# Attention of two batches ahead of all blocks, in rounds with three pairs under way, and the blocks of two chunks in alternation

## The chip, the cores and the metric

One core of a Trainium2 chip runs the program. The metric is the device time of one execution in microseconds (us), lower is better. "The second layer starts" is used below as a second, finer metric: it is the first matmul record of the second layer of chunk 0, up to which both kernels do the same work and after which their programs are alike.

In the views PE is TensorE (matmuls), PEld its weight loads, DVE VectorE, ACT ScalarE, and L159 is line 159 of that kernel, so the same statement can have another number in another kernel. PSUM is the memory into which all matmuls of this kernel write. "Half clock" means that the trace's record of the granted TensorE clock reads 0.50; in the two traces the record changes after 3.41 us or a multiple of it. The head pairs of attention go through steps that are called KV, Q, U, NORM and X below.

## The reference, cut to what matters

```python
def _attn_ref(q, k, v, g_norm):                 # batch 8, heads 8, seq 576, head_dim 64, fp32
    kv = np.einsum('bhsd,bhse->bhde', k, v)
    out = np.einsum('bhsd,bhde->bhse', q, kv)
    rms = np.sqrt(np.mean(out * out, axis=-1, keepdims=True) + 1e-06)
    return out / rms * g_norm

def _moe_ref(x, w_gate, w_val, w_out):          # x: 4608 x 512, d_ff 1536
    gate = 1.0 / (1.0 + np.exp(-(x @ w_gate)))
    return gate * (x @ w_val) @ w_out
```

The weights come as 64-bit floats. The kernel loads them as pairs of 32-bit words and converts them on the chip, unit by unit: 12 units of gate and value weights, 6 of output weights.

## The kernel before

Tokens are cut into chunks of 512. A chunk's first layer has 12 blocks (one for each 128 columns of d_ff), and a block (c, f) needs weight unit f. Chunk 0 needs the four head pairs of batch 0. Chunk 1 needs batch 1 as well. The code is shortened.

```python
def convert(u): return [s0, s1, s2, s3, s4, s5, s6]   # seven DVE steps for one weight unit; L159 is in s6;
                                                      # s2 also starts ACT's Abs of the next unit

def attention(n, at_ps):                              # one head pair, eleven steps
    # kv_mm (PE), kv_out (DVE, then load k, v of pair n+2), q_mm (PE transpose), q_out (ACT copy, then load q),
    # u_mm (PE), u_square (ACT), u_sum (DVE), u_root (ACT Sqrt), u_norm (DVE), x_mm (PE transpose), x_out (ACT)
    ...

load_unit(0)                                          # first loads
for n in range(2):
    load_kv(n)
    load_q(n, nc.scalar)
...
do(0, KV, KV_OUT, Q, Q_OUT)                           # batch 0: hardly two pairs under way
do(1, KV, KV_OUT, Q, Q_OUT)
load_unit(1)
do(0, U, U_SQUARE, U_SUM, U_ROOT, U_NORM)
do(2, KV, KV_OUT, Q, Q_OUT)
do(0, X, X_OUT)
...
for f in range(1, NHP + 2):                           # blocks (0,1)..(0,5), one pair of batch 1 inside each
    plain(0, f, 7, pair_steps(f - 1))
for f in range(NHP + 2, NFT):                         # then alternating, six units apart
    plain(0, f, 5, [[]] * 8)
    plain(1, f - NHP - 2, 5, [[]] * 8)
for f in range(NFT - NHP - 2, NFT - 3):
    plain(1, f, 8, [[]] * 8)
finish()
convert_some(len(converts))
second_layer(0, two, 2)
```

## Time and profile before

| | before |
|---|---|
| median of the runs beside the change | 1215.49 us (1212.87 to 1215.98, 4 runs) |
| PE busy | 1172.0 us, 97% of 1213.0 |
| PE idle before 113 us / from there to 220.6 us | 32.7 us / 0.1 us |
| second layer starts | 220.63 us |

A PE that is busy 97% of the time leaves little to gain, so the reader should ask where the other 3% lie, and where it is busy at half its clock. Both lie in the first 113 us (granted clock 0.91 from 14 to 51 us, 0.86 from 51 to 113, then 1.00). The lines for it are in the prediction.

### The profile page before, as it was taken

The numbers are of one execution on the slowest core, as the hardware profiler recorded it, in microseconds if no ns is written. First come the engines' busy times: TensorE is split into PE (matmuls) and PEld (weight loads), VectorE is DVE, ScalarE is ACT, GpSimd is POOL, SyncE is SP. The second block draws the span as 40 slices with busy tenths as digits, with TensorE's granted clock in tenths as the row PEclk, the third lists the DMA queues.
The fourth block names the chain that finished last, engine by engine and source line by source line (L and its number), as shares of the span: only waits on it lengthen the run. The fifth ranks groups of instructions, "written<-read, shape, count | busy, mean of one in ns | idle before, by whom it ended". The sixth has DMA issues, their size and how long they took to land.

```text
span 1213.0 us, 13391 instructions
## 1 busy us (share of the span) xinstructions
PE 1172.0 (97%) x5136; PEld 786.9 (65%) x5136; DVE 473.5 (39%) x845; ACT 308.5 (25%) x577; POOL 241.8 (20%) x342
## 2 busy tenths in 40 slices
PE   4788999999999999999999999999999999999998
PEld 4444444455478846885588648874888478748863
DVE  4667878303034412543045404540345125504430
ACT  3444121113033312431143203420334021101110
POOL 0000000100024401331044203330244015403410
PEclk9889999999999999999999999999999999999999
DMA  9544322131012101120211102110110000010000
GB/s 243 136 129 134 104 104 70 29 78 46 17 47 60 30 18 47 31 59 9 56 30 31 38 26 59 30 31 26 40 29 1 18 18 1 1 27 9 1 9 26
DMA packets 71582, 57.48 MB, mean 47 GB/s; under 512 B 40800, under 2 KB 65376, under 8 KB 71520
## 3 DMA queue, kind: packets, MB, share of 16 engines
q1 hardware_dynamic: 68992, 56.05, 17.0%
q10 hardware_dynamic: 2528, 0.59, 0.3%
q8 instruction: 41, 0.67, 0.2%
q14 instruction: 21, 0.17, 0.0%
HBM read 47.19 MB, written 9.44 MB: 47 GB/s over the span
## 4 chain that ended last, share of the span: by engine, by line
PE 93%; DVE 3%; ACT 2%; DMA 1%; issue 1%; ACTq 0%; SPq 0%; DVEq 0%
PE mm L489 42%; PE mm L321 23%; PE two L341 13%; PE two L321 7%; PE at L238 2%; PE two L238 2%; PE at L211 1%; PE at L264 1%; DVE sq L256 1%; PE at L224 1%; PE two L211 1%; DMA q<-in_q_dram 1%; ACT L251 1%; PE two L264 1%; DVE ms L247 1%; ACT sq L243 1%
## 5 line engine op out<-in xcount | busy, mean ns | idle before, releaser
L472 POOL TENSOR_TENSOR tw<-gv 128x256 f32<-128x256 f32 x168 | 120.4, 728 | 913.8 <-PE mm L489 691.5
L321 PE MATMUL mm<-wo,gv 128*128 128x512 f32 x672 | 290.5, 592 | 0.0
L489 PE MATMUL mm<-sx,tw 128*128 128x256 f32 x1008 | 234.2, 380 | 0.0
L321 PEld LDWEIGHTS mm<-wo,gv 128*128 128x128 f32 x672 | 127.3, 190 | 155.3 <-issue 155.0
L489 PEld LDWEIGHTS mm<-sx,tw 128*128 128x128 f32 x1008 | 188.8, 190 | 24.6
L341 PE MATMUL two<-xT,gv 128*128 128x512 f32 x384 | 176.7, 611 | 14.3 <-DVE gv L159 14.3
L501 DVE TENSOR_TENSOR gv<-mm,p 128x256 f32<-128x256 f32 x84 | 35.7, 425 | 321.2 <-PE mm L489 321.2
L489 PE MATMUL mm<-xT,gv 128*128 128x256 f32 x672 | 159.7, 380 | 1.2 <-ACT sg L326 1.2
L489 PEld LDWEIGHTS mm<-xT,gv 128*128 128x128 f32 x672 | 126.0, 190 | 21.2 <-issue 2.9
L341 PEld LDWEIGHTS two<-xT,gv 128*128 128x128 f32 x384 | 72.2, 195 | 98.2 <-issue 93.1
L472 POOL TENSOR_TENSOR tw<-gv,tw 128x256 f32<-128x256 f32 x168 | 126.2, 771 | 1.1
L321 PE MATMUL two<-wo,gv 128*128 128x512 f32 x192 | 84.6, 594 | 0.0
L326 ACT COPY sg<-mm 128x512 f32<-128x512 f32 x28 | 16.4, 585 | 264.5 <-PE mm L321 264.5
L510 DVE TENSOR_TENSOR gv<-mm,p 128x256 f32<-128x256 f32 x84 | 35.6, 424 | 114.3 <-PE mm L489 114.3
L489 PE MATMUL mm<-sx,gv 128*128 128x256 f32 x336 | 79.9, 381 | 0.0
L489 PE MATMUL mm<-xT,tw 128*128 128x256 f32 x336 | 79.9, 381 | 0.0
L519 ACT ACTIVATE sg<-sg 128x256 f32<-128x256 f32 x84 | 35.0, 417 | 162.9 <-DVE sg L518 161.6
L489 PEld LDWEIGHTS mm<-xT,tw 128*128 128x128 f32 x336 | 63.0, 190 | 8.5
L489 PEld LDWEIGHTS mm<-sx,gv 128*128 128x128 f32 x336 | 63.0, 190 | 8.5
L526 DVE TENSOR_TENSOR gv<-gv,sg 128x512 f32<-128x512 f32 x84 | 66.6, 832 | 0.2
L321 PEld LDWEIGHTS two<-wo,gv 128*128 128x128 f32 x192 | 35.8, 190 | 41.8 <-issue 41.6
L495 ACT COPY p<-mm 128x256 f32<-128x256 f32 x84 | 31.3, 372 | 93.5 <-PE mm L489 93.5
(67 smaller groups left out, 824.7 us busy)
## 6 DMA issues: line engine op xcount, KB each, us to landing
k<-in_k_dram SPq DMA_DIRECT2D x32, 288.0 KB, 3.5
v<-in_v_dram SPq DMA_DIRECT2D x32, 288.0 KB, 4.1
q<-in_q_dram SPq DMA_DIRECT2D x60, 144.0 KB, 3.1
st<-in_moe_w_gate_dram SPq DMA_DIRECT2D x12, 512.0 KB, 3.9
st<-in_moe_w_val_dram SPq DMA_DIRECT2D x12, 512.0 KB, 5.1
st<-in_moe_w_out_dram SPq DMA_DIRECT2D x12, 512.0 KB, 4.1
out_dram<-sg SPq DMA_DIRECT2D x24, 192.0 KB, 2.3
out_dram<-sg SPq DMA_DIRECT2D x24, 128.0 KB, 2.3
```

The costliest lines, as they stand in the source:

```text
L211: nc.tensor.matmul(ps[HD * e:HD * e + HD, 0, 0:HD], pairs[n]["k"][:, e, js], pairs[n]["v"][:, e, js], start=(j == 0), stop=(j == NJ - 1))
L238: nc.tensor.matmul(ps[0:NP, j // JH, c0:c0 + P], d["qT"][:, j // JH, NP * (j % JH):NP * (j % JH) + NP], kvs[n % 2], start=True, stop=True)
L264: nc.tensor.transpose(ps[:, j // JH, c0:c0 + NP], d["xn"][:, j // JH, P * (j % JH):P * (j % JH) + P], ident[0:NP, 0:NP])
L321: nc.tensor.matmul(ps[:, i], gv[c, f][:, ts], w["wo", f], start=(f == 0), stop=(f == NFT - 1))
L341: nc.tensor.matmul(self.ps[:, i], w[("wg", "wv")[i], self.f][:, m, :], xT[self.c][:, m, :], start=(m == 0), stop=(m == NMT - 1), skip_grou ...
L472: nc.gpsimd.tensor_tensor(out=tw[f, i], in0=b[in0], in1=b[in1] if isinstance(in1, tuple) else tw[f, in1], op=ALU.subtract)
L489: nc.tensor.matmul(ps, wt[:, m, :], xs[:, m, :], start=(new and m == 0), stop=(m == NK - 1), skip_group_check=True)
L495: nc.scalar.copy(out=d["p1"], in_=pa)
L501: tt(out=d["h"][:, h1], in0=pb, in1=d["p1"], op=ALU.add)
L510: tt(out=d["h"][:, h2], in0=pb, in1=d["p1"], op=ALU.add)
L519: nc.scalar.activation(out=d["sg"][:, h2], in_=d["sg"][:, h2], func=AF.Sigmoid)
L526: tt(out=d["h"], in0=d["h"], in1=d["sg"], op=ALU.mult)
```

## The change

The intent is to take the weight conversion out of PE's way. The attention of batches 0 and 1 is done first, in rounds in which three pairs are under way, from PSUM buffers of its own. Then the blocks of chunks 0 and 1 alternate, so that one weight unit serves two blocks in a row. The first loads are reordered too.

```diff
+    load_kv(0)
+    load_q(0)
     load_unit(0)
-    for n in range(2):
-        load_kv(n)
-        load_q(n, nc.scalar)
+    load_kv(1)
+    load_q(1)
 ...
+    def early(kind):
+        shape, bufs = {"kv": ([P, 1, 512], 2), "qx": ([P, 2, 512], 1), "u": ([P, 2, 512], 2)}[kind]
+        return psum_e.tile(shape, FP32, tag=kind, name=kind, bufs=bufs)
 ...
+    def stage(i, n_convert):
+        do(i, KV, KV_OUT, Q, Q_OUT)
+        do(i - 2, U_SUM, U_ROOT, U_NORM)
+        do(i - 3, X, X_OUT)
+        do(i - 1, U, U_SQUARE)
+        ...
+    for i in range(NE + 1):
+        stage(i, 3 if i < 2 else 1 if i == 2 else 0)
+    blk = Plain(0, 0, early("u"))
+    for m in range(NMT):
+        blk.mm(0, m)
+    take_abs(1)
+    stage(NE + 1, 1)
+    for m in range(NMT):
+        blk.mm(1, m)
+    stage(NE + 2, 1)
+    blk.gate()
+    convert_some(1)
+    blk.end()
+    psum_ctx.__exit__(None, None, None)
     psum0_ctx = tc.tile_pool(name="psum0", bufs=4, space=bass.MemoryType.PSUM)
 ...
-    for f in range(1, NHP + 2):
-        plain(0, f, 7, pair_steps(f - 1))
-    ...
+    plain(1, 0, 7)
+    for f in range(1, NFT - 3):
+        plain(0, f, 6)
+        plain(1, f, 6)
+    for f in range(NFT - 3, NFT):
+        plain(0, f, 6)
```

More of the change, by code (lines that the diff above doesn't have):

```diff
@@ L71, in load_kv, with load_q @@
             pairs[n][name] = t
-    def load_q(n, queue=None):
+    def load_q(n):
         if n >= B * NHP:
@@ L78, in load_q @@
         for e in range(2):
-            (queue or nc.sync).dma_start(out=t[:, :, e, :], in_=q[b, h0 + e].rearrange("(p j) d -> p j d", j=NJ))
+            nc.sync.dma_start(out=t[:, :, e, :], in_=q[b, h0 + e].rearrange("(p j) d -> p j d", j=NJ))
         pairs[n]["q"] = t
@@ L206, in kv_mm @@
         def kv_mm():
-            d["kv"] = ps = at_ps()
+            d["kv"] = ps = at_ps("kv")
             for j in range(NJ):
@@ L220, in q_mm @@
         def q_mm():
-            d["q"] = ps = at_ps()
+            d["q"] = ps = at_ps("qx")
             for j in range(NJ):
@@ L232, in u_mm @@
         def u_mm():
-            ps = at_ps()
+            ps = at_ps("u")
             d["u"] = ps[0:NP, :, 0:JH * P]
@@ L260, in x_mm @@
         def x_mm():
-            d["x"] = ps = at_ps()
+            d["x"] = ps = at_ps("qx")
             for j in range(NJ):
@@ L327, in second_layer, with two, __init__ @@
                 store(c, t0 + i, ot)
-    def two():
+    def two(kind=None):
         return psum0.tile([P, 2, 512], FP32, tag="two", name="two")
+    def early(kind):
+        shape, bufs = {"kv": ([P, 1, 512], 2), "qx": ([P, 2, 512], 1), "u": ([P, 2, 512], 2)}[kind]
+        return psum_e.tile(shape, FP32, tag=kind, name=kind, bufs=bufs)
     class Plain:
-        def __init__(self, c, f):
-            self.c, self.f = c, f
-            self.ps = two()
+        def __init__(self, c, f, ps):
+            self.c, self.f, self.ps = c, f, ps
         def mm(self, i, m):
@@ L355, in finish, with plain @@
             late.popleft()()
-    def plain(c, f, n_convert, steps=None):
+    def plain(c, f, n_convert):
         converted(f)
-        blk = Plain(c, f)
+        blk = Plain(c, f, two())
         for at in range(2 * NMT):
@@ L363, in plain @@
             blk.mm(i, m)
-            if steps:
-                for step in steps[at]:
-                    step()
-            if steps is None:
-                slot()
+            slot()
             if late:
@@ L372, in plain, with do @@
         late.extend([blk.gate, blk.end])
+    KV, KV_OUT, Q, Q_OUT, U, U_SQUARE, U_SUM, U_ROOT, U_NORM, X, X_OUT = range(11)
+    psum_ctx = tc.tile_pool(name="psum_e", bufs=1, space=bass.MemoryType.PSUM)
+    psum_e = psum_ctx.__enter__()
+    NE = 2 * NHP
+    a = [attention(n, early) for n in range(NE)]
+    def do(n, *steps):
+        if 0 <= n < NE:
+            for step in steps:
+                a[n][step]()
+    def stage(i, n_convert):
[3 more added lines that the diff above has]
+        do(i - 1, U, U_SQUARE)
+        if i == 0:
+            take_abs(0)
+        convert_some(n_convert)
+        if i + 2 == NE:
+            load_unit(1)
+            load_unit(2)
@@ L374 @@
+    for i in range(NE + 1):
[12 more added lines that the diff above has]
+    psum_ctx.__exit__(None, None, None)
     psum0_ctx = tc.tile_pool(name="psum0", bufs=4, space=bass.MemoryType.PSUM)
     psum0 = psum0_ctx.__enter__()
-    a = [attention(n, two) for n in range(2 * NHP)]
@@ L378, in do @@
-    def do(n, *steps):
-        for step in steps:
-            a[n][step]()
-    KV, KV_OUT, Q, Q_OUT, U, U_SQUARE, U_SUM, U_ROOT, U_NORM, X, X_OUT = range(11)
-    take_abs(0)
-    converted(0)
-    do(0, KV, KV_OUT, Q, Q_OUT)
-    do(1, KV, KV_OUT, Q, Q_OUT)
-    load_unit(1)
-    do(0, U, U_SQUARE, U_SUM, U_ROOT, U_NORM)
-    do(2, KV, KV_OUT, Q, Q_OUT)
-    do(0, X, X_OUT)
-    do(1, U, U_SQUARE, U_SUM, U_ROOT, U_NORM)
-    do(3, KV, KV_OUT, Q, Q_OUT)
-    load_unit(2)
-    do(1, X, X_OUT)
@@ L395 @@
-    do(2, U, U_SQUARE, U_SUM, U_ROOT, U_NORM)
-    blk = Plain(0, 0)
-    for i in range(2):
-        blk.mm(i, 0)
-    do(2, X, X_OUT)
-    do(3, U, U_SQUARE, U_SUM, U_ROOT, U_NORM)
-    for m in (1, 2):
-        for i in range(2):
-            blk.mm(i, m)
-    take_abs(1)
-    do(3, X, X_OUT)
-    converted(1)
-    do(4, KV, KV_OUT, Q)
-    for i in range(2):
-        blk.mm(i, 3)
-    do(4, Q_OUT)
-    late.extend([blk.gate, blk.end])
-    def pair_steps(p):
-        n, o = a[NHP + p] if p < NHP else None, a[NHP + p - 1] if p else None
-        slots = [[] for _ in range(2 * NMT)]
-        if n:
-            if p:
-                slots[0] += [n[KV]]
-                slots[1] += [n[KV_OUT], n[Q]]
-                slots[2] += [n[Q_OUT]]
-            slots[3] += [n[U]]
-            slots[4] += [n[U_SQUARE]]
-            slots[5] += [n[U_SUM]]
-            slots[6] += [n[U_ROOT]]
-            slots[7] += [n[U_NORM]]
-        if o:
-            slots[2] += [o[X]]
-            slots[3] = [o[X_OUT]] + slots[3]
-        return slots
@@ L432 @@
-    for f in range(1, NHP + 2):
-        plain(0, f, 7, pair_steps(f - 1))
-    for f in range(NHP + 2, NFT):
-        plain(0, f, 5, [[]] * 8)
-        plain(1, f - NHP - 2, 5, [[]] * 8)
-    for f in range(NFT - NHP - 2, NFT - 3):
-        plain(1, f, 8, [[]] * 8)
+    plain(1, 0, 7)
[4 more added lines that the diff above has]
+        plain(0, f, 6)
     finish()
@@ L556, in mm_ps, with at_ps @@
         return psum.tile([P, 512], FP32, tag="mm", name="mm", bufs=6)
-    def at_ps():
+    def at_ps(kind):
         return psum.tile([P, 2, 512], FP32, tag="at", name="at")
```

## The prediction

> **What bounds the kernel now.** I read first the page: PE is busy 97% of 1213 us, so only the stretch where it is not can pay. The busy time by stage finds that stretch.
>
> ```profile
> 0.00:14.00 14.00, 2.70 (x30) 2.32 (x30) 5.66 (x9) 2.95 (x3) 0.70 (x6) 1.00 0.88 213
> 14.00:51.00 37.00, 26.59 (x209) 20.50 (x209) 18.76 (x31) 16.41 (x31) 0.00 (x0) 0.91 0.77 178
> 51.00:113.00 62.00, 50.98 (x232) 27.50 (x233) 42.42 (x56) 26.23 (x36) 0.00 (x0) 0.86 0.49 142
> 113.00:220.60 107.60, 107.54 (x253) 47.46 (x251) 89.16 (x96) 22.12 (x29) 1.72 (x3) 1.00 0.26 88
> 220.60:338.00 117.40, 116.83 (x433) 57.16 (x431) 15.45 (x28) 22.43 (x40) 3.88 (x6) 1.00 0.17 44
> ```
>
> Columns: stretch, length, busy time of PE, PEld, DVE, ACT, POOL, granted clock, DMA share, GB/s. PE idles 11.3 + 10.4 + 11.0 us before 113 us and nowhere after, and the clock is below full only there. Next, the timeline of PE gives prices and the moment at which I shall compare.
>
> ```profile
> 113.01 107.78 PE L341 MATMUL two<-xT,gv 128*128 128x512 f32 x250
> 220.63 1.88 PE L321 MATMUL two<-wo,gv 128*128 128x512 f32 x4
> 222.44 0.92 PE L211 MATMUL two<-v,k 96*64 96x64 f32 x24
> 223.29 3.70 PE L321 MATMUL two<-wo,gv 128*128 128x512 f32 x8
> 226.83 0.66 PE L224 MATMUL two<-ident,q 96*128 96x96 f32 x6
> 227.32 3.63 PE L321 MATMUL two<-wo,gv 128*128 128x512 f32 x8
> 230.78 1.47 PE L238 MATMUL two<-kv,qT 128*96 128x128 f32 x12
> 232.09 2.31 PE L321 MATMUL two<-wo,gv 128*128 128x512 f32 x5
> ```
>
> 250 records in 107.78 us are 0.431 us each; the code's 8 matmuls of a block are 16 records (384 for 24 blocks), so a block costs 6.90 us. From start to next start KV costs 0.85, Q 0.49, U 1.31 and the second transpose X the same as Q: 3.15 us a pair. Up to 220.63 us, where the second layer of chunk 0 begins, both kernels do the same PE work: 21 blocks (12 of chunk 0, 9 of chunk 1) and 8 pairs, 145 + 25 = 170 us. The kernel before wastes 50.5 us by then. After that point the programs are equal. So the question is only when this point comes.
>
> The waits of PE up to 330 us tell what it waits for:
>
> ```profile
> PE two L341 <- DVE gv L159: 14.3, 5, 3.2
> PE two L211 <- DMA v<-in_v_dram: 11.8, 2, 10.7
> PE two L264 <- DVE sq L256: 5.0, 4, 2.1
> ```
>
> L159 is the last of seven DVE steps that convert one weight unit; blocks 0 to 5 of chunk 0 each need a fresh unit, and DVE has attention to do as well. The other waits are the first loads and the latency of a pair's norm, since hardly two pairs are under way. They sum to 31 us; the rest of the 50.5, some 19, is chiefly half clock.
>
> [...] the granted clock falls to 0.91 and 0.86 just where PE has gaps; 24 KV matmuls take 1.55 us early and 0.92 later. [...] The trace has the switches, at 1.28 us each:
>
> ```profile
> 57.75 0.81 ACT L243 ACTIVATE sq<-two 96x768 f32<-96x768 f32 x1 [5.76 <-PE two L238]
> 58.57 1.28 ACT L251 ACT_TABLE_LOAD   x1
> 59.86 0.30 ACT L251 ACTIVATE ms<-ms,eps 96x12 f32<-96x12 f32 x1
> 60.19 1.28 ACT L346 ACT_TABLE_LOAD   x1
> 61.48 0.60 ACT L346 ACTIVATE sg<-two 128x512 f32<-128x512 f32 x1
> ```
>
> [...] q moves in pieces of 256 B; the trace shows only 223 to 259 GB/s between 10 and 40 us with its DMA share at 1. I use 240 GB/s for pairs and 330 for weight units.
>
> **The change, part by part.**
>
> (1) *Loads reordered.* k, v, q of pair 0 come before the first weight unit. A pair is 864 KB, 3.6 us; a unit 1.05 MB, 3.2 us. Data flows from 2 us. Pair 0 is there by 6, its KV and Q run (cold) until 8.6; then unit 0 to 9.0 and pair 1 to 12.6[...]. Since U of pair 0 stands behind KV and Q of pair 1 in PE's order, the gain of the start is partly lost: round 1 runs from 13 to 18 us at half clock.
>
> (2) *Rounds.* A round is KV, Q, X of three pairs ago, U of the last. The one buffer for Q and X makes PE wait for the ACT copy of Q: 0.64 us and two hand-overs of 0.15, 0.93 in all. Period: 3.15 + 0.93 + some 0.25 for ends not overlapped = 4.35 us. ACT (0.64 + 0.30 + 1.04 + 0.81 = 2.8) and DVE (0.45 + 0.95 + 0.22 + 0.95 = 2.6) lie beside it. [...] DMA: 8 pairs, unit 0 and unit 3 (issued when unit 0 is converted) are 9.0 MB; paced by the two buffers, pair 5 lands near 31 to 32, pair 7 near 39. Rounds 2 to 7 go 18 to 44, with half a microsecond lost to DMA near round 5.
>
> (3) *The tail, stages 8 to 10 with block (0,0).* X and U: 1.8 us, to 46. The block takes a buffer of U that NORM of pair 6 must free: about 2 us, to 48. Then two halves of 3.45 us and two X of 0.5: PE is through at 55.7.
>
> (4) *Hand-over of PSUM.* The early pool is closed and the old one opened, so plain(1,0) may have to wait for everything in the early pool, that is for the end of block (0,0): XOUT of pair 7 1.0, table load 1.28, sigmoid 0.60, multiply 0.69, so near 59.3. In the kernel before, the next such hand-over shows PE waiting 1.16 us for the last copy out of the closed pool, whichever buffer that was. I take the wait, 3.6 us, and 1.5 us of half clock after it.
>
> (5) *Blocks.* 20 remain, 138 us. DVE per block: 6 steps (a unit's seven take 7.1 us, so 6.1) + 0.61 for the multiply = 6.7 us against 6.90 of PE. Tight, but with four PSUM buffers and an alternation that needs a unit only every 13.8 us, DVE does not hold PE up: by block (0,f), 5+12f steps have been issued and 7(f+1) are needed. All 126 steps are out by the last block. Five of the table switch pairs vanish, but beside other work.
>
> Sum: 59.3 + 1.5 + 138 = 198.8 us for the start of the second layer, against 220.6. The gain is 21.8 us: 1215.4 - 21.8 = 1193.6. With chance of a cheaper hand-over (4) I put it at 1192.5 us.
>
> **The rivals.**
>
> *A. Hand-over is free.* Then plain(1,0) starts at 55.7, but unit 1 is ready only after the multiply at 59.3 and four steps of 4.5 us, at 64, so block (0,1) waits 1.4 us. Second layer at 195: 1190. For it: per-buffer release is possible. Against: the wait of 1.16 us.
>
> *B. DVE becomes the bound of the block stage.* 6.7 of 6.9 leaves 0.2 us a block. If each step comes 5% dearer, 20 blocks cost 0.1 us more each, and any wait for the sigmoid adds; second layer near 203 to 208, so 1198 to 1203. For it: DVE is busy 89 of 107.6 us already with fewer steps a block. Against: PE waits for nothing in that stage now.
>
> *C. Half clock or DMA holds the rounds.* Cold, a pair costs PE some 6.4 us, a round 7.3: six rounds would take 18 us more and leave almost no gain, 1210. For it: from 10 to 34 us the clock of the kernel before toggles. Against: its PE was idle nearly a third of that time, the rounds under a quarter. Half of this fear is the upper end of my range.
>
> **Range and chances.** A gives 1190, the sum 1193.6, B 1200, half of C 1203; a start 3 us quicker than I think gives 1186. Eight in ten: 1184 to 1204. The 2% line is 1191.1, close below my figure: faster 0.41, same 0.57, slower 0.02.
>
> **What would show it.** In the profile after: the first L321 record at 199 us (195 to 206); the sigmoid switch only once before 60 us; round period of 4.3 us by successive KV starts from 20 to 44 us, with KV records of 0.92 us; a PE gap of 2 us before block (0,0) and of 3 to 4 before the second block, released by L349's multiply; then no PE wait for L159 over 1 us. Rounds of 6 us or more, KV at 1.5 us, or PE gaps before every second block would prove the working wrong; so would a changed stretch from the first L321 to the end, which I hold at 992 us.

The sum came to 59.3 + 1.5 + 138 = 198.8 us. Behind unit 0 the trace of the kernel before has 0.1 us from landing (7.24 us) to the DVE step that waits for it (7.34). That a round takes 4.35 us was the estimate. Other estimates, with what the same trace has:

- 240 GB/s for pairs and 330 for units: 223 to 259 between 10 and 40 us, and 330 from 51.06 to 54.48 us, while a unit is loaded.
- 1.5 us of half clock after the hand-over: 8 records behind a wait of 3.24 us took 5.37 us, later ones 3.60.
- 6.4 us for a pair in rival C: its records at half clock add up to 6.1 (KV 1.48, Q 1.01, U 2.65, X 0.98).

## The result

| | before | after |
|---|---|---|
| median | 1215.49 us | 1198.28 us (1196.88 to 1199.55, 4 runs) |
| ratio | | 0.9862, 95% interval 0.9844 to 0.9881: the same at 2%, though clearly a little faster |
| second layer starts | 220.63 us | 203.56 us |
| from there to the end of the span | 992.4 us | 992.4 us |

A ratio is the mean time of one kernel's runs over that of the other's of the same rounds, so it is not quite the ratio of the medians quoted.

The gain is all in front of the second layer: 17.1 us there and 17.1 us in the span. The busy time by stage of the changed kernel (columns as in the prediction) shows where:

```profile
0.00:14.00 14.00, 4.09 (x54) 3.71 (x54) 3.42 (x8) 3.07 (x3) 0.70 (x6) 1.00 0.95 227
14.00:51.00 37.00, 29.64 (x322) 26.80 (x318) 22.09 (x39) 19.67 (x41) 0.00 (x0) 0.91 1.10 244
51.00:113.00 62.00, 58.05 (x137) 25.98 (x138) 49.15 (x54) 16.91 (x24) 0.00 (x0) 0.94 0.36 107
113.00:203.56 90.56, 90.56 (x213) 40.09 (x212) 81.74 (x89) 17.91 (x22) 3.86 (x6) 1.00 0.30 100
```

Between 14 and 51 us the changed kernel fits 322 matmul records where the kernel before fits 209, with the DMA share at 1.10 against 0.77. Between 51 and 113 us PE idles 4.0 us instead of 11.0. The waits of PE up to 330 us (engine, tile and line, what it waited for, us in total, times, longest) say what went and what came:

```profile
PE kv L212 <- DMA v<-in_v_dram: 9.9, 2, 5.3
PE qx L265 <- ACT qT L230: 3.9, 5, 0.8
PE two L345 <- DVE gv L353: 3.8, 1, 3.8
PE u L345 <- DVE sq L257: 1.8, 1, 1.8
```

The 14.3 us of waiting for weight conversion (L159) are gone. Waiting for the first loads shrank from 11.8 to 9.9 us. Three waits are new: the copy of Q in each round, the norm of pair 6 before block (0,0), and one of 3.8 us for L353, the multiply that ends block (0,0). All waits before the second layer (with three smaller ones not shown) fell from 32.8 to 21.1 us, that is by 11.7.

The rest is clock. The trace's record of the granted clock has, between 20 and 113 us, 23.9 us at half clock in the kernel before and 13.7 in the changed one. PE was busy 23.2 and 12.9 us of that. Half of it is lost (an estimate from the record of 0.50; at the hand-over, the comparison with e1_gate_early below gives 3.1 of 6.2 us), 11.6 against 6.5 us, a gain of 5.1. Together 11.7 + 5.1 = 16.8 of the 17.1 us. This is one trace of each kernel, but the mean clock on record for the timed runs goes the same way: 0.994 to 0.996 in the eight of the changed kernel, 0.987 to 0.994 in those of the kernel before.

Timeline of PE after: of rounds 4 to 7 (counted from 0, as in `stage(i)`) the KV records alone, then the tail and the hand-over:

```profile
25.29 0.92 PE L212 MATMUL kv<-v,k 96*64 96x64 f32 x24
31.93 0.92 PE L212 MATMUL kv<-v,k 96*64 96x64 f32 x24
38.74 0.92 PE L212 MATMUL kv<-v,k 96*64 96x64 f32 x24
43.04 0.92 PE L212 MATMUL kv<-v,k 96*64 96x64 f32 x24
```

```profile
51.10 3.67 PE L345 MATMUL u<-xT,gv 128*128 128x512 f32 x8 [1.83 <-DVE sq L257]
54.61 0.66 PE L265 MATMUL qx<-ident,sq 96*128 96x96 f32 x6
55.10 3.62 PE L345 MATMUL u<-xT,gv 128*128 128x512 f32 x8
58.57 0.66 PE L265 MATMUL qx<-ident,sq 96*128 96x96 f32 x6
63.08 17.47 PE L345 MATMUL two<-xT,gv 128*128 128x512 f32 x33 [3.85 <-DVE gv L353]
```

From one KV to the next is one round: 6.64, 6.81 and then 4.30 us. The two long rounds are those with half clock. The windows of the clock, laid over the busy time, show it (the second number of a line is the length, the third PE's busy time, the third from the end the granted clock):

```profile
24.89:28.30 3.41, 2.04 (x35) 1.57 (x33) 2.95 (x6) 2.55 (x6) 0.00 (x0) 1.00 1.11 320
28.30:31.71 3.41, 3.34 (x17) 3.34 (x18) 1.38 (x3) 1.36 (x5) 0.00 (x0) 0.50 1.22 225
31.72:35.13 3.41, 1.82 (x33) 1.38 (x31) 1.39 (x3) 1.48 (x3) 0.00 (x0) 1.00 1.20 228
35.13:38.54 3.41, 3.39 (x18) 3.39 (x18) 1.18 (x2) 1.21 (x4) 0.00 (x0) 0.50 1.18 229
38.54:41.95 3.41, 2.63 (x41) 2.22 (x41) 1.79 (x5) 1.86 (x4) 0.00 (x0) 1.00 0.51 114
48.78:52.20 3.42, 1.58 (x8) 0.92 (x7) 2.61 (x4) 2.86 (x6) 0.00 (x0) 1.00 1.10 314
```

A window in which PE was busy 60% or 53% was followed by one at half clock. After one with 77% the clock stayed full. But the share of busy time alone does not decide it: the last line, with the wait before block (0,0) in it, has 46%, and the clock stayed full until 62.44 us. What the record of the clock goes by is not shown by these runs.

### The profile page after: what moved, and what is told of

It is laid out like the page before. It is cut to its first block, busy times and chain, and to the rows that moved or that the text cites. A ratio compares the mean times of both kernels' runs of the same rounds, so it can differ in the third digit from the quotient of the medians.

```text
span 1195.9 us, 13384 instructions
## 1 busy us (share of the span) xinstructions
PE 1166.5 (98%) x5136; PEld 785.7 (66%) x5136; DVE 474.2 (40%) x845; ACT 298.6 (25%) x569; POOL 242.0 (20%) x342
## 3 DMA queue, kind: packets, MB, share of 16 engines
q1 hardware_dynamic: 71360, 56.64, 17.9%
## 4 chain that ended last, share of the span: by engine, by line
PE 95%; ACT 2%; DMA 2%; DVE 1%; issue 0%; SPq 0%; ACTq 0%; DVEq 0%
PE mm L471 42%; PE mm L322 23%; PE two L345 14%; PE two L322 7%; PE at L239 2%; PE at L212 1%; PE at L265 1%; PE at L225 1%; PE u L239 1%; DMA q<-in_q_dram 1%; ACT L252 1%; DMA v<-in_v_dram 1%; PE u L345 1%; DVE sq L257 0%; PE two L239 0%; PE qx L225 0%
## 5 line engine op out<-in xcount | busy, mean ns | idle before, releaser
L322 PEld LDWEIGHTS mm<-wo,gv 128*128 128x128 f32 x672 | 127.3, 190 | 155.3 <-issue 155.0
L345 PE MATMUL two<-xT,gv 128*128 128x512 f32 x368 | 162.8, 602 | 3.8 <-DVE gv L353 3.8
```

The lines of the kernel that those rows point to most:

```text
L322: nc.tensor.matmul(ps[:, i], gv[c, f][:, ts], w["wo", f], start=(f == 0), stop=(f == NFT - 1))
L345: nc.tensor.matmul(self.ps[:, i], w[("wg", "wv")[i], self.f][:, m, :], xT[self.c][:, m, :], start=(m == 0), stop=(m == NMT - 1), skip_grou ...
```

## The experiments

Twelve runs follow: ten edits of the changed kernel, one of them run twice, and the changed kernel once more. Each was right against the reference. "Last U" is the start of the last U of attention (pair 7); the columns "last U" to "between" are from the profiled run. "Half-clock windows" counts windows of 3.4 us at half clock from 20 us to the last U. The runs were made in four groups, each with the kernel before beside it (e1 to e4; e5 to e7; e8, e9 and the two repeats; e10), so across groups the ratios compare better than the medians.

| run | half-clock windows | last U | second layer | between | median of all runs | ratio to before |
|---|---|---|---|---|---|---|
| changed kernel | 2 | 47.79 | 203.56 | 155.8 | 1198.28 | 0.9862 |
| after_again | 1 | 47.04 | 202.76 | 155.7 | 1197.43 | 0.9866 |
| e1_gate_early | 1 | 46.69 | 196.70 | 150.0 | 1191.35 | 0.9814 |
| e2_per_buffer | 1 | 46.05 | 196.19 | 150.1 | 1192.06 | 0.9822 |
| e3_old_loads | 3 | 51.91 | 206.28 | 154.4 | 1198.07 | 0.9866 |
| e4_old_blocks | 2 | 48.37 | 212.99 | 164.6 | 1208.38 | 0.9945 |
| e5_two_pairs | 6 | 62.71 | 212.64 | 149.9 | 1207.09 | 0.9951 |
| e6_filler | 0 | 44.84 | 200.16 | 155.3 | 1197.64 | 0.9870 |
| e6_filler_again | 1 | 49.23 | 204.75 | 155.5 | 1197.81 | 0.9862 |
| e7_unit_later | 2 | 45.35 | 200.46 | 155.1 | 1196.11 | 0.9863 |
| e8_unit_later_2 | 1 | 44.08 | 203.17 | 159.1 | 1197.34 | 0.9853 |
| e9_best | 1 | 44.33 | 198.32 | 154.0 | 1193.84 | 0.9830 |
| e10_tail | 3 | 51.05 | 198.21 | 147.2 | 1193.72 | 0.9833 |

### Which part of the change brings the gain

**e3_old_loads**: the first loads as in the kernel before (cut: `load_q` gets its argument for the queue back).

```diff
-    load_kv(0)
-    load_q(0)
     load_unit(0)
-    load_kv(1)
-    load_q(1)
+    for n in range(2):
+        load_kv(n)
+        load_q(n, nc.scalar)
```

> The changed kernel with the first loads in the order of the kernel before (weight unit 0 first, q on the ACT queue). First KV at 10.7 instead of 5.3, KV of pair 1 at 14.5 instead of 12.6. Theory: only the second of these counts, since round 1 stands behind pair 1, so the second layer comes up to 2 us later, at 205.5. Rival: the start is worth what the first matmul gained, 5.4 us, so 209.

The first KV moved from 5.30 to 10.51 us, the second from 12.61 to only 13.61, and the timed runs show no difference: 1198.07 us here, 1198.28 and 1197.43 for the changed kernel. The second layer of the one profiled run lies 2.7 us later, but that run was the slowest of its four and had three half-clock windows in its rounds. The reordered loads bring nothing that these runs can show; a gain of a microsecond would be lost in their spread. That the early start leads nowhere because round 1 waits for pair 1 fits the trace, where the second KV moved by only 1.0 us.

**e4_old_blocks**: blocks in the old order, attention as changed.

```diff
-    plain(1, 0, 7)
-    for f in range(1, NFT - 3):
-        plain(0, f, 6)
-        plain(1, f, 6)
-    for f in range(NFT - 3, NFT):
-        plain(0, f, 6)
+    for f in range(1, NHP + 2):
+        plain(0, f, 7)
+    for f in range(NHP + 2, NFT):
+        plain(0, f, 5)
+        plain(1, f - NHP - 2, 5)
+    for f in range(NFT - NHP - 2, NFT - 3):
+        plain(1, f, 8)
```

> The changed kernel with the blocks in the order of the kernel before (six of chunk 0, then alternating), attention as changed. Theory: the alternation is what keeps PE from waiting for weight conversion: without it each of blocks (0,1) to (0,5) waits, some 4.4 us at the first and 0.8 at each later one, 7 to 8 us in all, second layer at 210 to 212, waits for L159 of 7 us. Rival: attention ahead of the blocks was the whole gain, DVE being free of attention converts fast enough, and the second layer stays within 1.5 us of 203.6.

The second layer starts at 212.99, 9.4 us later, and the median is 10 us up. The first line of its waits of PE:

```profile
PE two L345 <- DVE gv L159: 12.0, 5, 8.2
```

The five waits for conversion were 8.23, 1.70, 0.56, 0.90 and 0.65 us. Of the first, 3.85 is the hand-over wait that the changed kernel has too, so the order of the blocks costs 8.2 us. Its half-clock stretch after the hand-over was also one window longer (10.2 us, not 6.8), which is some 1.7 us more (an estimate, half of 3.41). Taking the alternation away therefore loses more than half of the gain, and the rival, that freeing DVE of attention is enough, is refuted.

**e5_two_pairs**: two pairs under way instead of three.

```diff
-        do(i - 2, U_SUM, U_ROOT, U_NORM)
-        do(i - 3, X, X_OUT)
-        do(i - 1, U, U_SQUARE)
+        do(i - 2, X, X_OUT)
+        do(i - 1, U, U_SQUARE, U_SUM, U_ROOT, U_NORM)
```

> The changed kernel with two pairs under way in a round (KV and Q of pair i, X of pair i-2, U and norm of pair i-1, the norm in the same round as its U). Theory: from the end of U to the norm's end is about 4 us of ACT and DVE, PE has only KV, Q and the copy of Q, 2.3 us, to put there, so each of some seven rounds gets about 1.7 us longer, and the bigger gaps bring half clock: second layer 10 to 18 us after 203.6. Rival: the rounds are paced by loads and the clock anyway, and two pairs do as well: within 3 us of 203.6.

```profile
PE qx L265 <- DVE sq L257: 15.7, 7, 3.7
```

PE waits 15.7 us for the norm. Four of the seven waits are 2.19 us long, and behind five of them the next U runs at half clock, wholly or in part (its 12 matmuls take 2.39 to 2.76 us; behind the other two 1.48): the last U comes 14.9 us later. Part of it is given back, because the edit also puts the last X ahead of the second half of block (0,0): its copy and the table load are over near 72.7 us (an estimate from the end of X at 70.33 and the 1.04 and 1.28 us that they took in the changed kernel), before that half ends at 73.79, and the hand-over wait is 1.41 us instead of 3.85. Block (0,0) has no norm to wait for either. The second layer is 9.1 us later. The third pair is worth as much as the alternation. The two numbers add up to more than the whole gain of 17.1, so they are not independent shares. The old order of blocks with two pairs under way was not run, so what is left to attention ahead of the blocks by itself stays open.

### Where the rest of the predicted gain went: the hand-over of PSUM

**e1_gate_early**: one line moved, so that ACT does the table load (1.28 us) and the sigmoid (0.60 us) of block (0,0) before the copy of the last pair and not behind it.

```diff
     for m in range(NMT):
         blk.mm(1, m)
-    stage(NE + 2, 1)
     blk.gate()
+    stage(NE + 2, 1)
     convert_some(1)
     blk.end()
```

> The changed kernel, with the sigmoid of block (0,0) put ahead of the last pair's X and copy on ACT, so that the early PSUM pool can close sooner. If the hand-over of PSUM (3.85 us of PE wait for the multiply of L353, then 6.8 us at half clock) is where my sum was short, the second block starts near 60.4 instead of 63.1 us, the wait falls to about 1.2 us, the half clock after it goes, and the second layer starts 2.7 to 6 us earlier than 203.6, at 197.7 to 201. Rival: the second block has to wait for the second weight unit or the clock anyway; then the second layer stays within 1 us of 203.6.

```profile
57.47 0.66 PE L265 MATMUL qx<-ident,sq 96*128 96x96 f32 x6
59.26 137.60 PE L345 MATMUL two<-xT,gv 128*128 128x512 f32 x320 [1.13 <-ACT xT L275]
196.70 1.88 PE L322 MATMUL two<-wo,gv 128*128 128x512 f32 x4
```

The wait shrinks from 3.85 to 1.13 us, as expected (the second layer comes at 196.70, a little ahead of the expected 197.7 to 201, as this run's rounds ended 1.1 us sooner too), and the clock stays full (1.00 from 55.1 to 65.3 us) through all 320 records of the 20 blocks: 137.4 us from their start to the second layer, where the changed kernel took 140.5. From the last U to the second layer it takes 150.0 us, 5.8 less. The time is 1191.35 us, ratio 0.9814 (0.9798 to 0.9830), which does not meet the changed kernel's 0.9844 to 0.9881. So the hand-over cost the change 5.8 us: 2.7 of wait and 3.1 of half clock after it.

**e2_per_buffer**: both early pools hand over buffer by buffer instead of as a whole.

```diff
-    psum_ctx = tc.tile_pool(name="psum_e", bufs=1, space=bass.MemoryType.PSUM)
+    psum_ctx = tc.tile_pool(name="psum_e", bufs=1, space=bass.MemoryType.PSUM, reuse_waits="tile")
 ...
-    psum0_ctx = tc.tile_pool(name="psum0", bufs=4, space=bass.MemoryType.PSUM)
+    psum0_ctx = tc.tile_pool(name="psum0", bufs=4, space=bass.MemoryType.PSUM, reuse_waits="tile")
```

> The changed kernel, with both early PSUM pools told to hand over buffer by buffer and not as a whole. My rival A: the second block starts at 59.2 without a wait, and the wait moves to the third block, which needs the second weight unit at about 67.4: 1.4 us there. Second layer at 198 if the clock stays full, 201 if not. If the wait is not due to the pool as a whole, nothing changes: 203.6.

```profile
57.33 7.06 PE L345 MATMUL two<-xT,gv 128*128 128x512 f32 x16
65.62 130.73 PE L345 MATMUL two<-xT,gv 128*128 128x512 f32 x304 [1.24 <-DVE gv L159]
```

The second block starts right behind the last transpose, and 1.24 us of the wait come back at the third block as a wait for unit 1 (1.4 expected). The clock stays full (304 records in 130.73 us, 0.430 each). This shows that the 3.85 us were the wait for the whole pool, and it plays the prediction's rival A on the chip.

### Half clock in the rounds, and the loads

**e6_filler**: half of U's matmuls done twice, in the gap that the copy of Q leaves (cut: `u_mm` takes the tile of the filler where there is one, and the list of steps grows by the filler, number 11).

```diff
+        def u_filler():
+            ps = d["ups"] = at_ps("u")
+            for j in range(3):
+                nc.tensor.matmul(ps[0:NP, 0, P * j:P * j + P], d["qT"][:, 0, NP * j:NP * j + NP], kvs[n % 2],
+                                 start=True, stop=True)
 ...
         do(i - 2, U_SUM, U_ROOT, U_NORM)
+        if 3 <= i < NE:
+            do(i - 1, 11)        # u_filler; u_mm then writes over the same tile
         do(i - 3, X, X_OUT)
```

> The changed kernel with half of U's matmuls done once more, for nothing, in the gap of 0.78 us in which PE waits for the copy of Q (rounds 3 to 7; U overwrites them). Theory: rounds 4 and 5 took 6.7 us instead of 4.3 because two 3.4 us windows [...] fell to half clock; with the gap filled no window between 24 and 45 us is at half clock, the gaps before X all but vanish, rounds stay at 4.3 to 4.5 us save for loads, and attention's last U ends 2 to 3.4 us earlier than at 49.3. Rival: the loads (0.82 us of wait in round 5) or the order of the rounds make the long rounds; the filler then changes nothing or costs up to 0.65 us a round.

The first trace looked like success: no half clock between 20 and 44 us (granted clock 1.00), last U at 44.84, second layer 3.4 us earlier. But its four times spread from 1194.34 to 1199.99 us. So it ran again beside the changed kernel itself:

> The filler once more, beside the changed kernel itself in the same rounds, since its four times spread from 1194 to 1200 while its trace gained 3.4 us. If half clock in the rounds costs the changed kernel 3 us on the average, the filler is 2 to 3.5 us faster than after_again; if that was the luck of one trace, under 1 us.

> The changed kernel again, as a control for the filler and the best version: 1197 to 1200 us, half-clock windows in the rounds in a number that differs from run to run.

The filler took 1197.81 us, the changed kernel 1197.43. Its second trace has a half-clock window at 36.1 us after all (the filler takes 1.38 us there, otherwise 0.82), and KV of pair 5 waits 2.11 us for its load. The gain of the first trace was luck. The filler does fill the gap (the waits for the copy of Q are gone in both of its traces), but it cannot fill a wait for loads.

**e7_unit_later**: weight unit 0, which is not needed before 51 us, loaded after pair 4.

```diff
-    load_kv(0)
-    load_q(0)
-    load_unit(0)
-    load_kv(1)
-    load_q(1)
+    for n in range(2):
+        load_kv(n)
+        load_q(n)
 ...
-        if i == 0:
+        if i == 2:
+            load_unit(0)
+        if i == 3:
             take_abs(0)
 ...
-        if i + 2 == NE:
+        if i + 3 == NE:
             load_unit(1)
             load_unit(2)
 ...
-        stage(i, 3 if i < 2 else 1 if i == 2 else 0)
+        stage(i, {4: 2, 5: 2, 6: 2, 7: 1}.get(i, 0))
```

> The changed kernel with the first weight unit loaded after pair 4 rather than after pair 0, unit 3 only after units 1 and 2, and unit 0 converted in rounds 4 to 7. Theory: the 4.6 us wait before the second KV is the load of a unit that is not needed before 51 us. Second KV near 9.5 instead of 12.6, rounds paced by PE, last U of attention at 43 to 45 instead of 49.3, second layer 4 to 6 us before 203.6. Rival: the loads in sum set the rounds, so what is taken from the front comes back as waits further on: second layer within 1.5 us of 203.6.

The second KV starts at 8.79 us instead of 12.61, but in round 4 PE waits 4.08 us for the copy of Q. On ACT that copy stood behind the Abs of unit 0, which waited for the load. This was a flaw of the edit, so **e8_unit_later_2** does the Abs one round later (`i == 4`) and converts in rounds 5 to 8.

> As e7_unit_later, with its flaw mended: there the absolute value of unit 0, on ACT, stood ahead of the copy of Q of pair 4 and waited for the unit's load, which held PE for 4.1 us and cost two windows at half clock. Now it stands one round later, and the conversion is in rounds 5 to 8. Theory: no wait for that copy over 0.8 us, last U of attention at 40 to 42, second layer at 195 to 197 (hand-over wait and its half clock still in it). Rival: the loads in sum set the rounds; then the waits come back as DMA waits and the second layer stays near 200.

```profile
28.00 0.92 PE L210 MATMUL kv<-v,k 96*64 96x64 f32 x24 [1.84 <-DMA v<-in_v_dram]
49.06 6.70 PE L343 MATMUL u<-xT,gv 128*128 128x512 f32 x8 [3.50 <-DVE gv L159]
```

The expectation missed. No wait for the copy of Q is over 0.80 us and the last U does come at 44.08, but KV of pair 5 now waits 1.84 us for its load, block (0,0) waits 3.50 us for the conversion of unit 0, and the block's first half then runs at half clock (6.70 us for 8 records instead of 3.67). The second layer starts at 203.17, as good as nothing gained. So the early load of unit 0 was no waste: it let DVE convert before PE needed the unit.

### Versions put together

**e9_best** joins e8, e1, e2, the filler, and block (0,0) in two KV banks instead of a U buffer. **e10_tail** leaves loads and rounds as they are and mends only the tail: e1, e2 and

```diff
-    blk = Plain(0, 0, early("u"))
+    halves = [early("kv") for _ in range(2)]
+    class Halves:
+        def __getitem__(self, at):
+            return halves[at[1]][:, 0]
+    blk = Plain(0, 0, Halves())
```

> The version that puts together what helped: unit 0 later (as mended), sigmoid of block (0,0) ahead of the last copy, PSUM handed over buffer by buffer, block (0,0) in two banks of the KV tag instead of a U buffer, and the filler in the rounds. Theory: the waits add: last U of attention at 40 to 41, no wait before block (0,0) save for the conversion of unit 0 near 43, second block at 51 without a gap, second layer at 188 to 190, 1180 to 1184 in all, a ratio of 0.971 to 0.976. Rival: conversion of unit 0 and 1 on DVE takes the place of the waits removed; second layer at 193 or later.

> The changed kernel with its loads and rounds as they are and only the tail mended: sigmoid of block (0,0) ahead of the last copy, PSUM handed over buffer by buffer, block (0,0) in two banks of the KV tag. Theory: the tail's waits are all that can be had without bringing in the conversion of unit 0: no PE wait between the last U of attention and the second layer above 0.5 us, no half clock after 45 us, second layer at 192 to 196 depending on the clock in the rounds, 1186 to 1190 in all, ratio 0.977 to 0.981. Rival: the conversion of unit 1 comes in the way of the third block, as in e2_per_buffer, and no more than e1_gate_early's 0.981 to 0.982 is reached.

e9_best missed by 10 us, and its rival came true: the wait for conversion, 3.41 us up to 49.22, and the half clock behind it (6.43 us for 8 records, 3.60 in e10_tail) took back what it saved. e10_tail did what was expected of the tail: the largest PE wait between the last U and the second layer is 0.36 us, and it takes 147.2 us for what takes 155.7 to 155.8 in the changed kernel. But its profiled run had three half-clock windows in the rounds, and its median over five rounds, 1193.72, missed the expected 1186 to 1190 and is no better than that of e1_gate_early. The lowest median, 1191.35 us, is that of e1_gate_early with one line moved. The interval of its ratio, 0.9798 to 0.9830, lies below that of the changed kernel, but overlaps those of e2, e9 and e10, so the order among these four is not shown.

## Why the prediction was right or wrong, point by point

The measured 1198.28 us lies inside the range of 1184 to 1204, and "within 2%" was held the likeliest. The point was 5.8 us too low: the gain was 17, not 23. The mechanism held; what was too small were two terms of the sum, the rounds and the half clock after the hand-over.

- **What bounds it and when it is over: right.** The second layer starts at 203.56 us; I named 199, and 195 to 206 as what would bear the working out. From there to the end it takes 992.4 us (992 held). PE does not wait for L159 any more, which was the core of the argument, and e4 shows that this takes the alternation.
- **(1) Loads: right.** First KV at 5.30 (6 held), second at 12.61 (12.6 to 13), round 1 over at 17.9 (18). That the early start is lost again is confirmed by e3, where nothing of it remains that the timed runs can show.
- **(2) Rounds: the mechanism right, the size wrong, and this is the larger error.** The step that failed is that the rounds would stay at full clock. An undisturbed round took 4.30 us (4.35 held). But two of the six full-clock windows between 18 and 45 us had only 53% and 60%, since a wait for ACT's copy of X (0.66 us) and one for q (0.82 us) came on top of the copy of Q (0.78 us), and each was followed by a half-clock window; wait and half clock lengthened the round by some 2.4 us in all. The first X of the tail begins at 47.25 where I had 44: 3.3 us. The prediction had named rounds of 6 us or more as proof against its working, and two came, of 6.64 and 6.81 us. That was rival C in a mild form, which I had kept for the upper end of the range alone. The argument against it rested on a misreading: from 10 to 34 us PE of the kernel before was idle 26% of the time (17.75 us busy of 24.00), not "nearly a third". The changed kernel was idle 19% from 18 to 44 us (21.16 busy of 26.00), and its clock toggled too. Six traces with the same loads and rounds (the changed kernel twice, e1, e2, e4, e10) have one to three such windows, and the last U between 46.05 and 51.05. A single trace of this stage says little.
- **(3) Tail: right.** The wait for NORM of pair 6 was 1.83 us (2 held), and from the first X of the tail to the end of the last one is 12.0 us (11.7 held).
- **(4) Hand-over: the wait right, what follows it too small.** 3.85 us, released by L353, the multiply that was named as L349 of the kernel before (3.6 held). The failed term is "1.5 us of half clock after it": two windows of half clock followed, not one, from 62.44 to 69.26, and cost 3.1 us by the comparison with e1. The chance of a cheaper hand-over, for which I took off 1 us, did not come. Rival A did not happen, though e2 shows it would have if the pool had been told so.
- **(5) Blocks: right.** No PE wait in 20 blocks. They took 140.5 us less the 3.1 of half clock, 137.4, against 138. Rival B did not happen. Four pairs of table switches vanish up to 330 us (7 loads of 1.28 us left of 15), not five; they were held to lie beside other work, and no run tests what this is worth.

In sum: 198.8 held, + 3.3 (rounds), + 0.3 (tail), + 0.25 (wait), + 1.6 (half clock after it), - 0.6 (blocks) = 203.6.

What stays open is why one run has one half-clock window in its rounds and another three. No run held all else equal and tested a cause.

## What to carry to other kernels

Where a fresh operand has to be prepared for every block, order the blocks so that each prepared operand serves two of them before the next is needed; this, and enough independent chains in flight to cover the slow chain of a norm, made the gain (taking away either put the second layer 9.4 or 9.1 us later). When two PSUM pools follow each other, look at what the last reader of the first one waits for on its own engine: one sigmoid queued behind a copy and a table load cost 5.8 us here, more than half of it as clock. Judge a stage full of short waits by several traces, not one.
